# Attention, routing and a sparse expert layer on one core: the last twelve attention tiles are moved into the leading expert's first run

## The chip, the core and the metric

The kernel runs on one NeuronCore of a Trainium2 chip. Its engines run side by side, each through its own queue of instructions in order: TensorE (PE; weight loads, PEld, overlap its matmuls), VectorE (DVE), ScalarE (ACT), GpSimd (POOL) and SyncE (SP, which here only issues DMAs). They wait for one another through semaphores. The metric is the time of one execution in microseconds; the time before is 616.67 us, the median of three runs (615.66 to 618.85).

## What is computed

The reference, shortened:

```python
# q, k, v: (8 batches, 8 heads, 576 tokens, 64), all float32
kv  = einsum('bhsd,bhse->bhde', k, v)
out = einsum('bhsd,bhde->bhse', q, kv)
x   = out / sqrt(mean(out**2, -1) + 1e-6) * g_norm   # then (4608 tokens, 512)
logits = x @ w_gate                                  # 8 experts
e_idx  = argmax(logits, axis=1)
gate   = softmax(logits)[e_idx];  eom = sigmoid(x @ w_output_gate)[e_idx]
y = gate * eom * (relu(x @ w1[e_idx]) @ w2[e_idx])   # w1: 512 x 1024, w2: 1024 x 512
```

Linear attention without a softmax, a normalisation for each head, and an expert layer in which every token goes to one expert.

## The kernel before

Tokens are worked on in 36 tiles of 128 (4.5 tiles to a batch). For each batch b, `kv_part` multiplies k and v in five pieces of rows (four of 128, loaded as `kvm`, and one of 64, `rem`), `kvT_part` transposes the result, and `m_part` multiplies it with the gate weights, so that a tile's product gives outputs and gate logits at once. `out_tile(g)` multiplies q of a tile with this (16 small matmuls in the trace for a tile in one batch, 32 for one that spans two), in a PSUM buffer of the pool `ps_b` (two buffers). ACT copies it out three times: `xrow` (the row for the expert layer), `sq` (squares) and `gp` (logits). `run_out` calls `out_tile` and, for the tile before, `sums` (DVE adds the squares); it then lets each routing generator that is under way go on by a step (`advance`).

`route(gi)` is such a generator, one for each group of tiles. On DVE it takes the root of the mean squares, scales and sums the logits, finds the expert and the gate; on PE it counts positions (`rps`); on DVE, ACT and POOL it builds one-hot places (`la`, `rrc`); on PE it adds them to tables of token numbers (`tblps`). The group that ends at tile 24 also names the expert with most tokens so far, the leading expert (`lead_expert`), and makes its list of rows (`lead_rows`, DVE).

Rows go to a table `xs` in DRAM (`xrow`, and the scales as `xtail`). An expert's run gathers its rows by index (`gather`, POOL), scales the heads (`scale_heads`, on POOL or DVE by `NORMS`), transposes them (`stage`: PE `tps`, ACT and DVE copy to `xT`), and multiplies with w1 (`mm1`, eight blocks `f` of 128 hidden units in `hps`, a buffer of `ps_b`; ACT and DVE write `hT`) and w2 (`mm2`, one output tile of 24 matmuls in `yps`). Each float32 operand is split into a high and a low part (`split`: ACT or DVE writes `whi`, DVE or POOL `wlo`), and a product is three matmuls.

The first run (run 0) takes the leading expert's 384 first rows, out of tiles 0 to 23, so that it can start before the routing is over; run 1 takes the rest of that expert (320 rows), runs 2 to 8 the other experts. Up to the end of the routing the order on each engine is that of the program (`manual_schedule` with `MAN`). It is set by hand: `p1_main` goes through the batches, `HOOKS` inserts steps after certain tiles and `TAIL` gives the steps after the last tile. Letters: R one routing step, L one step of the lead run (`lead_run`: a split, three `stage`, a split, eight `mm1`), S a split of w2, G the gather of run 0, Q the last sums. Before, all loads of attention come first on SP, in slots of 512 KB (30 slots, three kept spare, which `xrow` shares); tile 35 is finished before the lead run's transposes, and run 0's output tiles follow in the main loop, with `stage` of run 1 between their matmuls. Where PE, ACT and DVE are in the main loop, SP's and POOL's order is set by the scheduler.

Of the kernel before, what the change touches and what calls it, by code (L numbers as in the profile page):

```python
# [45 lines left out]
GR = (10, 10, 4, 12)  # L46
# [15 lines left out]
SPARE = 3  # L62
# [18 lines left out]
NORMS = ("PPP", "VPVP")  # L81
# [49 lines left out]
MAN = {ET.PE, ET.Activation, ET.DVE, ET.Pool}  # L131
# [3 lines left out]
def body(ctx: ExitStack, tc: tile.TileContext, kvm, rem, qT, wg, gn, w1, w2, kc, xs, tab, out):  # L135
# [30 lines left out]
    free = list(range(SLOTS))  # L166
    held = {}

    def take(shape, dt, name):
# [157 lines left out]
    def mm2(i, k, events):  # L327
# [5 lines left out]
        ps = ps_y.tile([P, DM], F32, name="yps", tag=f"y{ny % 2}")  # L333
        ny += 1
# [18 lines left out]
        y = hp.tile([P, DM], F32, name="y", bufs=3)  # L353
# [11 lines left out]
        tc.add_to_no_dep_group("out", i_.ins)  # L365

# [81 lines left out]
    def load(spare):  # L448

        while loads and len(free) > spare:  # L450
            where, k, src = loads.pop(0)
            n = src.shape[0]
            if k in where:
                nc.sync.dma_start(out=where[k][P - n:], in_=src)
                continue
            t = take([P] + list(src.shape[1:]), F32, "ld")
            nc.sync.dma_start(out=t[:n], in_=src)
            where[k] = t

    def kv_part(b):  # L460
# [4 lines left out]
        for s in range(5):  # L465
            for p in range(NP):
# [9 lines left out]
        for c in range(4):  # L476
            give(kvt.pop((b, c)))
        if b % 2:
            give(rt.pop(b // 2))
# [3 lines left out]
        return cp  # L483
# [31 lines left out]
    def out_tile(g):  # L515
# [19 lines left out]
        for p in range(NP):  # L535
            for b, r0, m in parts:
                q0 = g % 2 * P + r0

                for u in range(2):
                    r = slice(u * D, (u + 1) * D)  # L540
                    nc.tensor.matmul(ps[r0:r0 + m, u, p * W:(p + 1) * W], qt[g // 2][r, p, q0:q0 + m],  # L541
                                     augs[b % 3][r, p, :], start=True, stop=True)
# [29 lines left out]
    def route(gi):  # L572
# [10 lines left out]
        def pause(k):  # L583
            for _ in range(WAITS.get((gi, k), 1)):
                yield 1
# [179 lines left out]

    def xwrite(g, o, i):
# [30 lines left out]
    def run_out(limit):  # L797
        nonlocal done_tiles
        if done_tiles < limit:
# [4 lines left out]
            advance()  # L804
            load(SPARE)
            if not loads and not opened[0]:
                open_rows(0)
            if lead_placed and opened[0] and (0, 1, 0) not in raw and (1, 0) not in wgt:
                for c in range(1):
                    wload(0, 1, c)  # L810
            for step in HOOKS.get(done_tiles, ""):
                act(step)

    def act(step):
        if step == "R":
            advance()
        elif step == "W":
            for c in range(4):
                wload(0, 2, c)
        elif step == "X":  # L820
            open_rows(1)
# [3 lines left out]
        elif step == "G":  # L825
            gather(0)
            behind.append(nc.gpsimd.memset(mark, 0.0))
            for c in range(1, 4):
                after_rows(wload(0, 1, c))
        elif step == "N":  # L830
            scale_rows(0)
        elif step == "S":
            next(lead2, None)
        else:
            next(lead, None)

    def p1_main():
        load(SPARE)
        for b in range(B):
            lim = tiles_ready(b - 1) if b else 0  # L840
            cp = kv_part(b)
            load(SPARE)
            run_out(lim)
            kvT = kvT_part(cp)
            run_out(lim)
# [4 lines left out]
        while done_tiles < NT:  # L850
            run_out(NT)
        for step in TAIL:
            act(step)
# [319 lines left out]
```

## Time and profile before

| | us |
|---|---|
| median of the runs | 616.67 (615.66 to 618.85) |
| the profiled execution | 620.81, its span 618.8 |
| PE busy in the span | 566.5 (92%), mean granted clock 0.931 |
| DVE, ACT, POOL busy | 263.2, 222.0, 164.0 |
| loads of q, k, v on SP | first 90 us or so, at about 400 GB/s |
| leading expert's gather, first matmul of run 0, first matmul of run 1 | 110.86, 122.74, 174.69 |

A row of the timeline has the start, the duration, the engine, the line of the program, the operation, output and inputs, the shape and a count of merged instructions; in brackets the idle time of the engine ahead of it and what ended that. The granted clock is the share of TensorE's full clock. Spans on POOL are rough. A float32 matmul appears as two in the counts of the trace.

### The profile page before, as it was taken

Reading aid. Unit: us, or ns where it says so; the run is one execution under the profiler, and the core shown is the slowest. Engines: PE = TensorE matmul, PEld = TensorE weight load, DVE = VectorE, ACT = ScalarE, POOL = GpSimd, SP = SyncE. Lnnn points to the kernel's source line nnn. Section 1 sums busy time; section 2 is a strip of 40 time slices with the busy share of each in tenths; the row PEclk is TensorE's granted clock in tenths of the full one; section 3 lists DMA queues with packets and bytes.
Section 4 is the critical chain, followed back from the end, with each engine's and each line's share of the span. In section 5 each row is a group of like instructions: output and inputs, shape, how many; then the busy total and the mean of one; then the engine's idle time right before and its main releaser. Section 6 shows DMA issues by size and latency. Waiting matters only on the chain.

```text
span 618.8 us, 10459 instructions
## 1 busy us (share of the span) xinstructions
PE 566.5 (92%) x4179; PEld 506.3 (82%) x4179; DVE 263.2 (43%) x536; ACT 222.0 (36%) x413; POOL 164.0 (27%) x163
## 2 busy tenths in 40 slices
PE   3799978848999999999899999999999999999991
PEld 3688868747898998889789988998799889889881
DVE  2123688699425456225331453235135325424300
ACT  1335545634225334323331343234234423523310
POOL 2001044443832510630036117104500630110010
PEclk9958777579999999999999999999999999999996
DMA  8999991770564622349776332524432451110010
GB/s 271 367 409 407 405 366 49 246 285 7 166 231 138 202 89 90 87 169 35 16 159 199 115 122 91 172 69 138 145 112 74 135 181 68 53 52 2 0 47 14
DMA packets 39122, 92.53 MB, mean 150 GB/s; under 512 B 14418, under 2 KB 14546, under 8 KB 39072
## 3 DMA queue, kind: packets, MB, share of 16 engines
q1 hardware_dynamic: 32176, 71.63, 37.4%
q0 software_dynamic: 6464, 20.00, 10.2%
q8 instruction: 34, 0.56, 0.4%
q10 hardware_dynamic: 432, 0.21, 0.1%
q14 instruction: 16, 0.13, 0.1%
HBM read 72.63 MB, written 19.99 MB: 150 GB/s over the span
## 4 chain that ended last, share of the span: by engine, by line
PE 57%; issue 19%; DMA 10%; DVE 4%; POOL 3%; ACT 3%; another core or an unknown queue 2%; SPq 0%; POOLq 0%; DVEq 0%
PE hps L308 24%; PE yps L350 23%; PE ops L541 3%; PE kvps L474 3%; DMA ld<-kvm 3%; DMA xs<-xrow 2%; PE tps L271 2%; POOL out L361 2%; DMA ld<-qT 2%; DMA ld<-rem 2%; PE yps L345 1%; POOL xg L239 1%; DMA wraw<-w 1%; DMA xg<-xs,gidx 1%
## 5 line engine op out<-in xcount | busy, mean ns | idle before, releaser
L308 PE MATMUL hps<-xT,whi 128*128 128x320 f32 (+4 forms) x1024 | 197.3, 310 | 9.5 <-DVE hT L318 8.4
L350 PE MATMUL yps<-whi,hT 128*128 128x512 f32 (+2 forms) x592 | 195.9, 399 | 1.0 <-ACT whi L221 1.0
L308 PEld LDWEIGHTS hps<-xT,whi 128*128 128x128 f32 x1024 | 163.6, 191 | 11.9 <-DVE hT L318 9.1
L350 PEld LDWEIGHTS yps<-whi,hT 128*128 128x128 f32 (+2 forms) x592 | 111.3, 188 | 25.2 <-ACT whi L221 1.2
L308 PE MATMUL hps<-xT,wlo 128*128 128x320 f32 (+4 forms) x512 | 121.6, 309 | 0.0
L318 DVE SCALAR_TENSOR_TENSOR hT<-hps,hT 128x512 fp32r<-128x512 f32 (+5 forms) x112 | 59.2, 529 | 142.6 <-ACT hT L317 142.3
L350 PE MATMUL yps<-wlo,hT 128*128 128x512 f32 (+2 forms) x296 | 116.6, 394 | 0.8 <-DVE wlo L224 0.8
L317 ACT ACTIVATE hT<-hps 128x512 fp32r<-128x512 f32 (+5 forms) x112 | 52.5, 469 | 164.0 <-PE hps L308 121.6
L308 PEld LDWEIGHTS hps<-xT,wlo 128*128 128x128 f32 x512 | 89.0, 191 | 0.0
L361 POOL DMA_INDIRECT out<-y,oidx x42 | 44.8, 1068 | 154.2 <-ACT y L360 107.2
L239 POOL DMA_INDIRECT xg<-xs,gidx x42 | 43.2, 1029 | 137.5 <-PE tps L271 54.6
L350 PEld LDWEIGHTS yps<-wlo,hT 128*128 128x128 f32 (+2 forms) x296 | 55.7, 188 | 12.1 <-DVE wlo L224 1.1
L217 DVE SCALAR_TENSOR_TENSOR wlo<-wraw,gcol,whi 128x1024 fp32r<-128x1024 f32 x32 | 43.9, 1372 | 39.6 <-ACT whi L214 39.6
L247 POOL TENSOR_TENSOR xg<-xg 128x512 f32<-128x512 f32 (+3 forms) x40 | 44.0, 1102 | 43.9 <-DMA xg<-xs,gidx 43.5
L541 PE MATMUL ops<-aug,ld 64*128 64x80 f32 (+1 forms) x640 | 49.0, 327 | 5.8 <-ACT gp L549 5.7
L541 PEld LDWEIGHTS ops<-aug,ld 64*128 64x128 f32 (+1 forms) x640 | 44.5, 230 | 8.8 <-ACT gp L549 6.4
L360 ACT ACTIVATE y<-yps,tl 128x512 f32<-128x512 f32 (+2 forms) x37 | 25.5, 689 | 71.4 <-PE yps L350 68.4
L276 ACT CAST xT<-tps 128x512 fp32r<-128x512 f32 (+3 forms) x45 | 23.6, 530 | 67.6 <-PE tps L271 63.9
L277 DVE TENSOR_TENSOR xT<-tps,xT 128x512 fp32r<-128x512 f32 (+3 forms) x45 | 27.7, 617 | 46.9 <-ACT xT L276 43.3
L474 PE MATMUL kvps<-ld 128*64 128x64 f32 (+1 forms) x640 | 36.4, 300 | 11.1 <-DMA ld<-kvm 10.7
L474 PEld LDWEIGHTS kvps<-ld 128*64 128x64 f32 (+1 forms) x640 | 33.1, 209 | 14.0 <-DMA ld<-kvm 12.0
L224 DVE TENSOR_TENSOR wlo<-wraw,whi 128x1024 fp32r<-128x1024 f32 x28 | 34.3, 1226 | 13.5 <-ACT whi L221 6.7
(158 smaller groups left out, 403.2 us busy)
## 6 DMA issues: line engine op xcount, KB each, us to landing
wraw<-w SPq DMA_DIRECT2D x64, 512.0 KB, 3.2
ld<-kvm SPq DMA_DIRECT2D x32, 512.0 KB, 10.2
ld<-qT SPq DMA_DIRECT2D x18, 512.0 KB, 10.2
xs<-xrow SPq DMA_DIRECT2D x13, 512.0 KB, 10.4
xs<-xrow SPq DMA_DIRECT2D x2, 1280.0 KB, 15.2
ld<-rem SPq DMA_DIRECT2D x3, 512.0 KB, 10.2
xg<-xs,gidx POOLq DMA_INDIRECT x42
out<-y,oidx POOLq DMA_INDIRECT x42
```

Source lines behind the costliest of these rows:

```text
L217: eng.scalar_tensor_tensor(out=lo, in0=r, scalar=gcol[:, 0:1], in1=hi.bitcast(F32), op0=ALU.mult, op1=ALU.subtract)
L224: eng.tensor_tensor(out=lo, in0=r, in1=hi.bitcast(F32), op=ALU.subtract)
L239: nc.gpsimd.indirect_dma_start(out=x[:M, :], out_offset=None, in_=rows, in_offset=bass.IndirectOffsetOnAxis(ap=gidx[:M, p, t:t + 1], axis=0))
L247: eng.tensor_tensor(out=v, in0=v, in1=f, op=ALU.mult)
L277: nc.vector.tensor_tensor(out=lo[:, :, c0:c0 + M], in0=v, in1=hi.bitcast(F32)[:, :, c0:c0 + M], op=ALU.subtract)
L308: nc.tensor.matmul(ps[:, j, :n], w[:, o:o + P], x[d][:, j * N:j * N + n], start=(d == 0 and k == 0), stop=(d == 3 and k == 2))
L317: nc.scalar.activation(hh, x, AF.Relu)
L318: nc.vector.scalar_tensor_tensor(out=v(h[:, l:l + n]), in0=x, scalar=0.0, in1=hh.bitcast(F32), op0=ALU.max, op1=ALU.subtract)
L350: nc.tensor.matmul(ps[:M], a, b, start=(f == 0 and k == 0), stop=(f == 7 and k == 2))
L361: i_ = nc.gpsimd.indirect_dma_start(out=out, out_offset=bass.IndirectOffsetOnAxis(ap=oidx[:M, p, t:t + 1], axis=0), in_=y[:M], in_offset=N ...
L474: nc.tensor.matmul(ps[u * D:(u + 1) * D, p * D:(p + 1) * D], k, v, start=(s == 0 and p == 0), stop=(s == 4 and p == NP - 1))
L541: nc.tensor.matmul(ps[r0:r0 + m, u, p * W:(p + 1) * W], qt[g // 2][r, p, q0:q0 + m], augs[b % 3][r, p, :], start=True, stop=True)
```

## The change

The first 24 tiles and batches 0 to 5 go through `p1_main` as before, but `kv_part` stops after the second and the fourth piece of rows and a tile is put there. Only their loads come first; the others (`later`) are issued between the row writes and then at the letters d and f of a new `SCRIPT`. This string takes the place of `HOOKS` and `TAIL` after tile 23: F finishes all routing that is open, 1 and 2 load pieces of w1 and w2, K, T, M are the three steps of a batch's kv product, o is one tile, X opens the row writes of tiles 24 and on, Y is one output tile of run 0. The groups of tiles are 8, 8, 8, 12 instead of 10, 10, 4, 12. Rows of tiles 0 to 23 have twelve slots of their own (`ROWS`), and the loads get the other 18 with none spare. Every tile is multiplied in pieces of 64 rows. Scaling of group 0's logits moves from POOL to DVE (`GPSIMD_GROUPS`), so does the scaling of run 0's rows (`NORMS`); the last group's logits are scaled and summed in halves (`APART`). Run 0's outputs use `ps_b` and slots; SP's order is also that of the program.

```diff
-GR = (10, 10, 4, 12)
+GR = (8, 8, 8, 12)
-SPARE = 3
+ROWS = LEAD_TILES // 2
-HOOKS = {15: 'R', 27: 'RR', 28: 'R', 31: 'RGW', 32: 'X', 34: 'NL'}
-TAIL = "QLLLLRRRSLSRRSLLRRRLSLRRSRLSLL"
-WAITS = {(0, 2): 3, (1, 7): 2, (1, 2): 0, (1, 8): 2, (1, 5): 0, (0, 8): 2, (0, 6): 2}
-GPSIMD_GROUPS = 1
-APART = (2,)
+FIRST = LEAD_TILES
+SCRIPT = ("fQF" "1G1" "K" "L" "T" "LLL" "dd" "1" "M" "L" "dd" "L" "Xo1o" "dd" "L" "o" "o" "dd" "L" "o" "dd" "o" "L" "K"
+          "22" "L" "T" "o" "22" "L" "M" "o" "S" "o" "o" "S" "o" "L" "S" "o" "o" "S" "Q" "L" "R" "L" "RR" "YRRR" "YRRR" "YRRRRRR")
+GPSIMD_GROUPS = 0
+APART = (2, 3)
-NORMS = ("PPP", "VPVP")
+NORMS = ("VVV", "VPVP")
-MAN = {ET.PE, ET.Activation, ET.DVE, ET.Pool}
+MAN = {ET.PE, ET.Activation, ET.DVE, ET.Pool, ET.SP}
-    free = list(range(SLOTS))
+    free = list(range(SLOTS - ROWS))
+    xfree = list(range(SLOTS - ROWS, SLOTS))
...
     def mm2(i, k, events):
-        ps = ps_y.tile([P, DM], F32, name="yps", tag=f"y{ny % 2}")
+        if i == 0:
+            ps = ps_b.tile([P, 2, 512], F32, name="yps0", tag="big")[:, 0]
...
     def kv_part(b):
         for s in range(5):
+            if s in (2, 4):
+                yield
...
     def out_tile(g):
-                for u in range(2):
-                    r = slice(u * D, (u + 1) * D)
-                    nc.tensor.matmul(ps[r0:r0 + m, u, p * W:(p + 1) * W], qt[g // 2][r, p, q0:q0 + m],
+                for c0 in range(r0, r0 + m, D):
+                    for u in range(2):
+                        r = slice(u * D, (u + 1) * D)
+                        nc.tensor.matmul(ps[c0:c0 + D, u, p * W:(p + 1) * W], qt[g // 2][r, p, q0:q0 + D],
...
     def route(gi):
         def pause(k):
-            for _ in range(WAITS.get((gi, k), 1)):
-                yield 1
+            yield 1
...
     def act(step):
+        elif step == "F":
+            while routing:
+                advance()
...
     def p1_main():
-        for b in range(B):
-            lim = tiles_ready(b - 1) if b else 0
-            cp = kv_part(b)
+        for b in range(B - 2):
+            lim = min(tiles_ready(b - 1) if b else 0, FIRST)
+            kv = kv_part(b)
+            for _ in range(2):
+                next(kv)
+                load()
+                run_out(lim)
...
-        while done_tiles < NT:
-            run_out(NT)
-        for step in TAIL:
+        while done_tiles < FIRST:
+            run_out(FIRST)
+        for step in SCRIPT:
             act(step)
...
             if i == 0:
                 gather(1)
                 scale_rows(1)
-                for _ in lead:
-                    next(lead2, None)
-                for _ in lead2:
-                    pass
+                for h in hT[0]:
+                    give(h)
+                for x in range(len(tiles_of(1))):
+                    stage(1, x)
+                continue
```

How the order on the engines moves, at three places. First, PE at the start of the lead run. Before, the last tiles (`ops`, here the end of tile 31 and tiles 32 to 35) stand ahead of run 0's transposes (`tps`) and first block (`hps`):

```order
L541 MATMUL ops<-aug_115,ld 64x80 x2
L541 MATMUL ops<-aug_116,ld 64x80 x2
L541 MATMUL ops<-aug_116,ld 128x80 x32
L271 MATMUL tps<-ident,xg 128x128 x12
L308 MATMUL hps<-xT,whi 128x384 x2
L308 MATMUL hps<-xT,wlo 128x384
```

After, the third group's table matmuls (`tblps`), the seventh batch's kv product and its transposes stand there:

```order
L767 MATMUL tblps<-rrc,la 128x96
L492 MATMUL kvps<-ld 64x64 x40
L507 MATMUL kvTps<-ident,kvc 128x128 x2
L274 MATMUL tps<-ident,xg 128x128 x12
L519 MATMUL mps<-gw,kvT 64x16 x8
L311 MATMUL hps<-xT,whi 128x384 x2
L311 MATMUL hps<-xT,wlo 128x384
```

Tiles 24 to 35 have moved behind the first block. On DVE at the same place, before, with the last index step of the routing (`oidx`), sums of squares (`ss`), the first split and the first tile's copies (`tl`, `xT`):

```order
L900 SCALAR_TENSOR_TENSOR oidx<-gif,zf 128x3
L562 TENSOR_REDUCE ss<-sq 128x8 x3
L216 TENSOR_SCALAR whi<-wraw,gcol 128x1024
L217 SCALAR_TENSOR_TENSOR wlo<-wraw,gcol,whi 128x1024
L562 TENSOR_REDUCE ss<-sq 128x8 x3
L267 COPY tl<-xg 128x1
L277 TENSOR_TENSOR xT<-tps,xT 128x2x128 x2
```

and after:

```order
L951 SCALAR_TENSOR_TENSOR oidx<-gif,zf 128x3
L500 COPY kvc<-kvps 128x256
L219 TENSOR_SCALAR whi<-wraw,gcol 128x1024
L220 SCALAR_TENSOR_TENSOR wlo<-wraw,gcol,whi 128x1024
L250 TENSOR_TENSOR xg<-xg 128x512
L270 COPY tl<-xg 128x1
L280 TENSOR_TENSOR xT<-tps,xT 128x2x128 x2
```

The sums have gone, the kv copy and the scaling of the gathered rows (`xg`, line 250) have come in. Second, PE at the last group's tables. Before, in the middle of run 0's first output tile (`yps`), with two blocks behind them:

```order
L350 MATMUL yps<-whi,hT 128x512 x2
L350 MATMUL yps<-wlo,hT 128x512
L350 MATMUL yps<-whi,hT 128x512
L749 LDWEIGHTS la
L749 MATMUL tblps<-rrc,la 128x96
```

After, the end of the tables is followed by run 0's third output tile:

```order
L767 LDWEIGHTS la
L767 MATMUL tblps<-rrc,la 128x96
L356 MATMUL yps_2252<-whi,hT 128x512
L356 MATMUL yps_2252<-wlo,hT 128x512
L356 MATMUL yps_2252<-whi,hT 128x512 x2
```

The tables have moved from the first output tile to between the second and the third. Third, the start of run 1. Before, its transposes stand between the matmuls of run 0's output tiles, behind run 0's last block:

```order
L308 MATMUL hps<-xT,whi 128x384 x2
L308 MATMUL hps<-xT,wlo 128x384
L271 MATMUL tps<-ident,xg 128x128 x4
L350 MATMUL yps<-whi,hT 128x512
L350 MATMUL yps<-wlo,hT 128x512
```

After, PE has them behind the last output tile:

```order
L356 MATMUL yps_2252<-whi,hT 128x512
L274 MATMUL tps<-ident,xg 128x128 x8
L274 MATMUL tps<-ident,xg 128x64 x4
L311 MATMUL hps<-xT,whi 128x320 x2
L311 MATMUL hps<-xT,wlo 128x320
```

and POOL's queue there, from the last group's places on, with gathers (`xg<-xs`) for runs 1 and 2, the scaling (line 250) and the third output tile's write (`out`):

```order
L737 TENSOR_SCALAR la<-ni,rlon 128x128 x4
L242 DMA xg<-xs,gidx 128x528 x2
L242 DMA xg<-xs,gidx 64x528
L242 DMA xg<-xs,gidx 128x528 x2
L250 TENSOR_TENSOR xg<-xg 128x512
L242 DMA xg<-xs,gidx 128x528
L367 DMA out<-y_2277,oidx 4608x512
```

Nothing of run 0 stands between run 1's transposes and its first block any more.

More of the change, by code (lines that the diff above doesn't have):

```diff
@@ L352, in mm2 @@
                 e()
-        y = hp.tile([P, DM], F32, name="y", bufs=3)
+        y = take([P, DM], F32, "y0") if i == 0 else hp.tile([P, DM], F32, name="y", bufs=3)
         if M == T:
@@ L365, in mm2 @@
         tc.add_to_no_dep_group("out", i_.ins)
+        if i == 0:
+            give(y)
     def lead_run():
@@ L446, in body, with load, fetch @@
                 nq += 1
[L448 to L458, printed above, removed]
+    cut = lambda w, k: (k if w is qt else 2 * k if w is rt else k[0])
+    later = [l for l in loads if cut(l[0], l[1]) >= (FIRST // 2 if l[0] is qt else FIRST * P // S + 1)]
+    loads = [l for l in loads if not any(l is x for x in later)]
+    later.sort(key=lambda l: (12.5 + (l[1] - FIRST // 2) // 2 if l[0] is qt else 2 * l[1] + 0.1 if l[0] is rt else 2 * l[1][0]))
+    def load():
+        while loads and free:
+            fetch(loads)
+    def fetch(loads):
+        where, k, src = loads.pop(0)
+        n = src.shape[0]
+        if k in where:
+            nc.sync.dma_start(out=where[k][P - n:], in_=src)
+            return
+        t = take([P] + list(src.shape[1:]), F32, "ld")
+        nc.sync.dma_start(out=t[:n], in_=src)
+        where[k] = t
     def kv_part(b):
@@ L475, in kv_part @@
                                      stop=(s == 4 and p == NP - 1))
[L476 to L479, printed above, removed]
+            if s < 4:
+                give(kvt.pop((b, s)))
+            elif b % 2:
+                give(rt.pop(b // 2))
         nc.scalar.copy(augs[b % 3][:, :, 0:D], ps[:, 0:NP * D].rearrange("q (p d) -> q p d", p=NP))
@@ L803, in run_out @@
                 sums()
-            advance()
-            load(SPARE)
+            if done_tiles <= FIRST:
+                advance()
+            load()
             if not loads and not opened[0]:
                 open_rows(0)
[L808 to L812, printed above, removed]
+            elif opened[0] and done_tiles <= FIRST and done_tiles % 2 == 0 and len(later) > LATER:
+                fetch(later)
+    w1s, w2s = list(range(4)), list(range(4))
+    state = {"b": B - 2}
     def act(step):
+        b = state["b"]
         if step == "R":
             advance()
[L817 to L821, printed above, removed]
+        elif step == "F":
+            while routing:
+                advance()
         elif step == "Q":
@@ L849, in p1_main @@
                 run_out(lim)
-        while done_tiles < NT:
-            run_out(NT)
-        for step in TAIL:
+        while done_tiles < FIRST:
+            run_out(FIRST)
+        for step in SCRIPT:
             act(step)
+        assert not later and done_tiles == NT and not w1s and not w2s and state["y"] == len(tiles_of(0))
         while routing:
             advance()
+        for _ in lead:
+            assert False
+        for _ in lead2:
+            assert False
     vec = nc.vector
@@ L1061, in body @@
                 mm2(i, k, at.get(k, {}))
-            if i == 0:
-                for h in hT[0]:
-                    give(h)
-            if i > 0:
-                for c in range(4):
-                    drop(2, c)
+            for c in range(4):
+                drop(2, c)
     main.close()
```

52 lines of the change are left out of this document (39 added, 13 removed).

## The prediction

> **What bounds the kernel now.** I read the stretches first (us: busy PE, PEld, DVE, ACT, POOL with counts; granted clock, DMA share, GB/s). They are cut where tile 23's square is done, where the leading expert's gather starts (110.9), where its first matmul starts (122.7) and where the second run's first matmul starts. The left-out row is 87.2 to 110.9. The second fence is the row of that matmul.
>
> ```profile
> 0.00:87.20 87.20, 68.83 (x1142) 61.75 (x1143) 32.73 (x84) 35.95 (x95) 12.05 (x18) 0.80 1.00 373
> ...
> 110.90:122.70 11.80, 9.76 (x74) 8.65 (x72) 8.17 (x15) 7.42 (x20) 7.26 (x7) 0.50 0.86 277
> 122.70:174.90 52.20, 41.52 (x209) 36.15 (x210) 36.76 (x81) 17.07 (x32) 28.95 (x24) 0.89 0.49 160
> 174.90:618.80 443.90, 428.45 (x2480) 383.17 (x2478) 164.31 (x270) 150.18 (x236) 108.24 (x102) 0.98 0.37 103
> ```
>
> ```profile
> 174.69 0.45 PE L308 MATMUL hps<-xT,whi 128*128 128x320 f32 x2
> ```
>
> From 174.9 on PE is busy 428.45 of 443.9 us, on work that the change leaves alone. So the question is when the second run's first matmul comes: at 174.69 now. Ahead of it PE is idle 10.7 us in the lead run (52.20 - 41.52), and 18.4 us in the first stretch, whose DMA share is 1.00. The change trades these holes for others. I follow the chain that ends in that matmul through five links.
>
> **Link 1, attention to tile 23.** Rows of ACT, PE, PEld and SP, a line of the waits (total, times, longest) and one of the issues (us to landing):
>
> ```profile
> 86.16 0.59 ACT L546 COPY xrow<-ops 128x512 f32<-128x512 f32 x1 [0.31 <-PE ops L541]
> 87.28 0.62 ACT L546 COPY xrow<-ops 128x512 f32<-128x512 f32 x1
> 79.56 4.07 PE L474 MATMUL kvps<-ld 128*64 128x64 f32 x77
> PE ops L541 <- ACT gp L549: 3.9, 5, 1.0
> 83.52 0.72 PE L541 MATMUL ops<-aug,ld 64*64 64x80 f32 x30
> 84.99 2.02 PE L541 MATMUL ops<-aug,ld 64*128 64x80 f32 x32
> 109.02 1.10 PEld L541 LDWEIGHTS ops<-aug,ld 64*64 64x64 f32 x32
> 110.29 5.20 PEld L541 LDWEIGHTS ops<-aug,ld 64*128 64x128 f32 x48 [0.17 <-issue]
> 50.07 2.89 SPq L457 DMA_DIRECT2D ld<-qT  x3
> ld<-qT SPq DMA_DIRECT2D x18, 512.0 KB, 10.2
> ```
>
> The first two rows are ACT's copies of tiles 23 and 24; tile 23 is through ACT by 87.2. The seventh batch's kv product (4.07, and 0.3 for its transposes) moves behind it: -4.4. Tiles set between the pieces of each kv product hide most of the 3.9 us in which PE's tiles wait for ACT: -3.0. Every tile takes the 64-row form that tile 22 has: 32 small matmuls in 0.8 us (30 take 0.72) against 1.01 (half of 2.02); at half clock 1.10 against 1.73 (a third of 5.20). The mean clock is 0.80, so two fifths of the time at half: 0.36 a tile, and -6.1 for the 17 tiles that don't wait for loads. Tile 23 is done at 73.7. Bounds: 82.8 if only the kv product goes; below, the loads of q that tiles 22 and 23 need are issued from 50.07 on and take 10.2, and some 7.5 us of kv and tile work follow: 67.8. The row writes now alternate with loads on SP's queue, where a write waits for its tile; what it can hold up is the seventh batch, not needed before link 3.
>
> **Link 2, the third group's routing, alone.** Now tiles 24 to 35 hide it. After, its matmuls stand on PE's queue ahead of the next kv product, so PE waits for DVE's chain. DVE's rows for the last group (twelve tiles), DVE's first step after the table matmuls of the present third group, and the gather on POOL:
>
> ```profile
> 134.76 1.76 DVE L618 TENSOR_TENSOR gp<-gp,xtail 128x1536 f32<-128x1536 f32 x1
> 138.09 2.80 DVE L622 TENSOR_REDUCE lg<-gp 128x192 f32<-128x1536 f32 x1
> 140.93 0.25 DVE L632 TENSOR_REDUCE mx<-lg 128x12 f32<-128x96 f32 x1
> 144.39 0.25 DVE L668 TENSOR_TENSOR rog<-ohb,lg 128x96 f32<-128x96 bf16 x1
> 146.12 0.16 DVE L704 TENSOR_TENSOR cnt<-rps,cf 128x8 f32<-128x8 f32 x1
> 147.72 0.75 DVE L729 TENSOR_TENSOR rrc<-cf,rhk 128x576 bf16<-128x576 f32 x1
> 150.08 0.18 DVE L742 TENSOR_TENSOR xtail<-rdn 128x12 f32<-128x12 f32 x1
> 109.13 0.26 DVE L890 TENSOR_TENSOR t<-tblps,perm 128x96 f32<-128x96 f32 x1 [0.41 <-PE tblps L749]
> 110.86 1.08 POOL L239 DMA_INDIRECT xg<-xs,gidx  x1 [5.09 <-DVE oidx L900]
> ```
>
> Small steps come every 0.25 us (0.25 busy at twelve tiles). For eight tiles, an estimate from these rows: the last square's sum and the rest of the second group 2.8; nine steps 2.3; scaling 1.3 and sums 2.0 (two thirds of 1.76 and 2.80, and two instructions for one); mask and its count 1.6; gate and slots 1.7 (146.12 - 144.39); leading expert, seven steps, 1.6; places 2.0 (2.4 at twelve, 147.72 to 150.08); table matmuls 0.6; table to gather 1.7 (110.86 - 109.13). Sum 17.6, bounds 15 and 20. Gather at 91.3, against 110.86.
>
> **Link 3, gather to first matmul**, 11.9 us now (110.86 to 122.74):
>
> ```profile
> 114.06 0.92 DVE L216 TENSOR_SCALAR whi<-wraw,gcol 128x1024 fp32r<-128x1024 f32 x1
> 124.63 1.28 DVE L217 SCALAR_TENSOR_TENSOR wlo<-wraw,gcol,whi 128x1024 fp32r<-128x1024 f32 x1 [0.62 <-ACT whi L214]
> 158.01 0.69 DVE L247 TENSOR_TENSOR xg<-xg 128x512 f32<-128x512 f32 x1 [1.66 <-DMA xg<-xs,gidx]
> 121.19 1.08 PE L271 MATMUL tps<-ident,xg 128*128 128x128 f32 x4 [1.62 <-DVE xT L277]
> 123.58 0.42 DVE L277 TENSOR_TENSOR xT<-tps,xT 128x256 fp32r<-128x256 f32 x1 [0.44 <-ACT xT L276]
> 122.74 1.15 PE L308 MATMUL hps<-xT,whi 128*128 128x384 f32 x2 [0.46 <-ACT xT L276]
> ```
>
> DVE will do in order: the copy of the kv product (on PE beside the gather; done some 3.5 us into it), the split (0.92 + 1.28), then three times scale, wait for the transposes, subtract. The scaling moves from POOL, where it ran ahead, onto this chain: 0.69 + (124.00 - 121.19) = 3.5 us a tile at half clock. 3.5 + 2.2 + 10.5 = 16.2, less 1.2 since the first matmul needs only half of the last tile's copies (122.74 against 124.00): 15.0, bounds 12 and 17. The first weight load is behind the third group's row tails on SP and lands inside these 3.5 us. First matmul at 106.3, 16.4 us earlier than now.
>
> **Link 4, the lead run with twelve tiles and the last kv product in it,** to the end of tile 35:
>
> ```profile
> 126.88 0.63 PE L308 MATMUL hps<-xT,whi 128*128 128x384 f32 x2
> 145.08 0.51 PE L308 MATMUL hps<-xT,whi 128*128 128x384 f32 x2
> 147.16 0.39 PE L350 MATMUL yps<-whi,hT 128*128 128x512 f32 x1
> ```
>
> PE: the first block of hidden units at half clock 4.1 (122.74 to 126.88), six more at 2.08 (145.08 to 147.16) 12.5, twelve tiles at 0.85 10.2, kv product, transposes and small product 4.7: 31.5. Tiles, blocks and small products share two PSUM buffers, so each waits until the job before the last is copied out. ACT needs 1.12 a tile (87.28 - 86.16), and its six splits stand between, each about as long as DVE's 1.28. Laid out job by job this leaves 4.9 us of holes; I add 1.0 for a clock that dips in the stretch of four tiles: 37.4, bounds 33 and 50. Tile 35 ends at 143.7. The last kvm loads wait on SP behind the rows of tiles 24 and 25, and have some 10 us until PE wants them.
>
> **Link 5, tile 35 to the second run.** Now most of the lead run's matmuls cover it; after, one block and three output tiles:
>
> ```profile
> 125.61 2.55 POOL L224 TENSOR_TENSOR wlo<-wraw,whi 128x1024 fp32r<-128x1024 f32 x1 [6.75 <-ACT whi L221]
> 125.83 2.39 DVE L589 TENSOR_SCALAR ra<-ss 128x96 f32<-128x96 f32 x1
> 161.93 5.48 PE yps L350 x24
> 154.18 3.80 DMA xg<-xs,gidx
> 129.00:137.00 8.00, 0.28 (x2) 0.00 (x0) 7.79 (x9) 1.92 (x3) 4.66 (x2) 0.81 0.81 296
> 137.00:140.50 3.50, 3.46 (x11) 3.46 (x12) 3.50 (x2) 0.00 (x0) 0.00 (x0) 0.50 0.00 0
> ```
>
> From tile 35's end: ACT and DVE drain, 3.7; the chain's first step sits beside POOL's last split and takes 2 us more, as at 125.83; routing at twelve tiles by the rows of link 2, 2.3 + 1.8 + 2.8 + 1.4 + 1.7 + 1.6 + 2.4 = 14.0; table matmuls 0.3; to the gather 2.0. That is 22.0. PE meanwhile has the last block (2.1) and two output tiles of 5.48, then waits some 6 us for the table matmuls, which stand ahead of the third output tile. That tile covers 5.5 us of what follows: POOL scales the middle tile behind five gathers (6.2, more than the 3.8 in which the first rows land), 1.1; transposes and copies 1.8; then the last tile is scaled on DVE, 0.7, and copied, 1.4. Together 33.2, bounds 28 and 38: second run at 176.9. PE has been idle some 8 us by then; after the idle 8.0 at 129 the clock was 0.50 for 3.5 us, which costs 1.7. So 178.6 against 174.69: **+3.9 us**. At nothing I put the rows' own slots and the lead output's shared buffers: loads are limited by the DMA share of 1.00, not by slots, and no tile wants a buffer beside the output.
>
> The profiled execution took 620.81 (span 618.8), 4.1 above the median of 616.67; I carry the difference over to the median: 620.6.
>
> **Rivals.** (a) Attention keeps the pace of the loads, because PE, fed without holes, gets the full clock. For it: the smaller form and the tiles between kv pieces. Against: PE was busy 9.76 of 11.80 us from 110.9, mostly with tiles, at 0.50. Tile 23 then ends at 67.8 (-5.9) and the dip in link 4 goes (-1.0): 613.7, faster. It decides only if tile 23 is done by about 68. [...]
> (b) Link 5 is covered better: the chain escapes POOL's split (-2.0) and the middle tile is scaled before the later gathers (-2.6): 616.0, no change. Against it: those gathers stand first on POOL's queue.
> (c) The clock stays at half through link 4: six blocks at 4.1 for 2.08, +12: 632.7. For it the same row at 0.50; against it 0.89 in the present lead run.
> (d) The lead run starts no earlier, so the change doesn't do what it says: row writes land late and hold the gather until 110. They are 6.3 MB behind 20 MB of loads, at 373 GB/s done near 75, so I give it little; link 1 to 3's 16.4 us lost: 637.
>
> **How the numbers follow.** My sum 42%, its own range 616 to 626; (a) 22%, (b) 20%, (c) 13%, (d) 3%. Half a per cent, 3.1 us, is about what a measurement here can tell from no change. Faster: most of (a), a third of (b): 0.27. Within: the rest of these and a third of my sum, which ends close to that line: 0.28. Slower: 0.45. For 8 in 10 the range goes past (a) to 609 and short of (c) to 631.
>
> **What would show it.** Tile 23 through ACT near 74; PE idle some 15 us behind it with DVE busy; gather near 91; first lead block near 106; tile 35 near 144; holes of about 6 us ahead of the third output tile and 8 behind it; second run near 177, and from there to the end the length of now. I am wrong if tile 23 comes by 68, if the lead run is at half clock, or if the stretch behind the second run's start changes.

## The result, and the profile after

| | before | after |
|---|---|---|
| median of the runs, us | 617.76 | 636.16 (632.48 to 637.32) |
| ratio after to before | | 1.0285, 95% interval 1.0225 to 1.0346 |
| the profiled execution, its span | 620.81, 618.8 | 637.32, 635.4 |
| mean granted clock | 0.931 | 0.937 |

The change makes the kernel 18.4 us slower; the forecast was 3.9 us, with a range that ended at 631. (All ratios below are against runs of the kernel before on the same chip and leave out runs more than 1.5% above the fastest of their kernel, five of twelve in early_tiles_2 and three of ten in early_tiles_4, whose medians over all runs are 616.77 and 611.39 against 616.75 and 617.75 before.)

First the stretches of the changed kernel, in the columns of the prediction's first fence (stretch and its length; busy PE, PEld, DVE, ACT, POOL with counts; granted clock, DMA share, GB/s). They are cut at the links' ends: tile 23's square, the leading expert's gather, run 0's first matmul, tile 35's last matmul, run 1's first matmul. The last line is the kernel before between its tile 23 and its gather, which the prediction left out.

```profile
0.00:82.70 82.70, 56.83 (x1385) 48.71 (x1385) 36.10 (x98) 35.22 (x93) 8.38 (x15) 0.86 0.98 355
82.70:100.90 18.20, 6.07 (x83) 5.02 (x85) 15.46 (x66) 3.10 (x12) 7.79 (x11) 0.56 0.17 43
100.90:114.50 13.60, 5.61 (x60) 4.04 (x56) 6.10 (x14) 2.61 (x7) 3.30 (x4) 0.63 0.88 306
114.50:151.10 36.60, 30.49 (x570) 26.43 (x566) 14.92 (x23) 22.85 (x51) 4.49 (x2) 0.94 0.60 216
151.10:187.70 36.60, 23.74 (x123) 19.23 (x123) 23.29 (x73) 10.21 (x22) 19.51 (x19) 0.90 0.51 162
187.70:635.40 447.70, 431.36 (x2480) 386.10 (x2480) 165.09 (x271) 149.69 (x235) 112.67 (x107) 0.98 0.37 99
```
```profile
87.20:111.00 23.80, 18.06 (x280) 16.66 (x281) 21.29 (x88) 11.53 (x35) 7.61 (x13) 0.69 0.41 118
```

The rows of the timeline that end the links, in order:

```profile
82.13 0.61 ACT L567 ACTIVATE sq<-ops 128x512 f32<-128x512 f32 x1
100.90 1.08 POOL L242 DMA_INDIRECT xg<-xs,gidx  x1 [4.94 <-DMA xs<-xtail]
150.29 0.78 PE L560 MATMUL ops<-aug,ld 64*64 64x80 f32 x32
174.66 1.08 POOL L242 DMA_INDIRECT xg<-xs,gidx  x1 [4.72 <-DVE oidx L951]
187.74 1.09 PE L311 MATMUL hps<-xT,whi 128*128 128x320 f32 x2 [0.46 <-ACT xT L279]
```

Run 1's first matmul is at 187.74, 13.05 us later than before (174.69). Behind it the changed kernel takes 447.7 us (635.4 - 187.74), the kernel before 444.1 (618.8 - 174.69): 3.55 more, which makes the 16.6 us between the two spans. Run 1's first block, dense matmuls, runs at half clock (0.50 granted) until 193.70, which costs 3.0 us of these; the same stretch took 441 to 448 us in the twelve kernels below, so a microsecond or two in it means little.

What fills the 13.05 us is idle TensorE. Up to run 1 as a whole it is idle 65.0 us for 36.8, and busy 122.7 for 138.1. From tile 23 to run 1 it is idle 18.2 - 6.07, 13.6 - 5.61, 36.6 - 30.49 and 36.6 - 23.74, in sum 39.1 us. Before, from 87.2 to 174.9, it was 5.7, 2.0 and 10.7, in sum 18.5. Ahead of tile 23 it was idle 18.4 us before and is 25.9 now.

By the prediction's links:

| link | predicted length (bounds for its end) | measured | miss |
|---|---|---|---|
| 1, attention to tile 23 | 73.7 (67.8 to 82.8) | 82.7 | +9.0 |
| 2, third group's routing | 17.6 | 18.2 | +0.6 |
| 3, gather to first matmul | 15.0 | 13.6 | -1.4 |
| 4, lead run to tile 35 | 37.4 | 36.6 | -0.8 |
| 5, tile 35 to run 1 | 33.2 | 36.7 | +3.5 |
| behind run 1's start | +1.7 | +3.55 | +1.9 |

Together these misses are 12.8 us, of the 14.5 that lie between +3.9 and +18.4; the rest is that the two profiled spans are 16.6 apart and the medians 18.4. Links 1 and 5 carry the miss, much of it in waits that the trace of before did not show. Here are link 1's waits, a line each for who waited for whom (total us, times, longest), up to 83 us:

```profile
PE kvps L492 <- DMA ld<-kvm: 8.6, 6, 5.4
PE ops L560 <- issue: 4.7, 3, 2.1
PE ops L560 <- ACT gp L568: 2.9, 3, 1.1
PE kvTps L507 <- DVE kvc L500: 2.5, 3, 1.1
PE tblps L767 <- POOL la L737: 1.7, 5, 0.4
```

The second line is new: TensorE stops inside a tile and waits for nothing that the profile shows, three times, 2.15, 2.04 and 0.46 us. I call such a stop, in a tile or in a batch's kv matmuls, a hole. The last line is a wait that `WAITS` had kept away: the first group's table matmuls stand on TensorE's queue while GpSimd still writes their places.

### The profile page after: what moved, and what is told of

It is laid out like the page before. It is cut to its first block, busy times and chain, and to the rows that moved or that the text cites. A ratio compares the mean times of both kernels' runs of the same rounds, so it can differ in the third digit from the quotient of the medians.

```text
span 635.4 us, 11490 instructions
## 1 busy us (share of the span) xinstructions
PE 554.1 (87%) x4691; PEld 489.5 (77%) x4691; DVE 261.0 (41%) x543; ACT 223.7 (35%) x417; POOL 156.1 (25%) x156
## 4 chain that ended last, share of the span: by engine, by line
PE 57%; issue 19%; DVE 6%; POOL 5%; DMA 5%; ACT 4%; another core or an unknown queue 1%; POOLq 0%; ACTq 0%; SPq 0%; DVEq 0%
PE hps L311 27%; PE yps L356 20%; PE kvps L492 3%; PE tps L274 3%; PE ops L560 2%; POOL out L367 2%; DMA ld<-kvm 2%; DMA ld<-qT 2%; POOL xg L242 1%; DMA wgs<-wg 1%; PE yps L351 1%; ACT sq L567 1%; ACT xrow L565 1%; POOL la L737 1%
## 5 line engine op out<-in xcount | busy, mean ns | idle before, releaser
L366 ACT ACTIVATE y<-yps,tl 128x512 f32<-128x512 f32 (+2 forms) x37 | 25.5, 689 | 82.2 <-PE yps L356 79.2
L250 POOL TENSOR_TENSOR xg<-xg 128x512 f32<-128x512 f32 (+3 forms) x37 | 40.6, 1101 | 40.7 <-DMA xg<-xs,gidx 40.4
L560 PE MATMUL ops<-aug,ld 64*64 64x80 f32 x1152 | 35.3, 263 | 14.0 <-ACT gp L568 5.0
L560 PEld LDWEIGHTS ops<-aug,ld 64*64 64x64 f32 x1152 | 28.4, 155 | 19.2 <-issue 10.0
L492 PE MATMUL kvps<-ld 128*64 128x64 f32 (+1 forms) x640 | 34.6, 283 | 8.8 <-DMA ld<-kvm 8.6
L274 PE MATMUL tps<-ident,xg 128*128 128x128 f32 (+3 forms) x168 | 26.7, 283 | 15.0 <-issue 5.9
```

Source lines behind the costliest of these rows:

```text
L250: eng.tensor_tensor(out=v, in0=v, in1=f, op=ALU.mult)
L274: nc.tensor.transpose(ps[:, c, :M], x[:M, c * P:(c + 1) * P], ident[:M, :M])
L492: nc.tensor.matmul(ps[u * D:(u + 1) * D, p * D:(p + 1) * D], k, v, start=(s == 0 and p == 0), stop=(s == 4 and p == NP - 1))
L560: nc.tensor.matmul(ps[c0:c0 + D, u, p * W:(p + 1) * W], qt[g // 2][r, p, q0:q0 + D], augs[b % 3][r, p, :], start=True, stop=True)
```

## Experiments on link 1

A link's end below is that of one profiled execution. Three kernels have the changed kernel's attention to the letter (the changed one, middle_tile_dve and weights_behind): tile 23 came at 82.7, 84.4 and 84.2. So a difference under 2 us in one such row says little.

**late_table.** The table matmuls of group 0 two tiles later:

```diff
+WAITS = {(0, 8): 3}
         def pause(k):
-            yield 1
+            for _ in range(WAITS.get((gi, k), 1)):
+                yield 1
```


> The changed kernel with one edit: the first group's table matmuls go onto TensorE's queue two attention tiles later, so that GpSimd's eight places (5.2 us) are done when TensorE comes to them. Theory 1 (the holes of link 1 are several separate waits, this one costs 2.6 us of idle TensorE between 65.7 and 68.8): tile 23 through ACT at 80.1 instead of 82.7, the second run at 185.1 instead of 187.7, the time 2.6 us shorter. Rival (TensorE waits for the loads or for ACT right behind it, so the wait only moves): tile 23 still at 82 to 83, time within 1 us.

Ratio 1.0287 (1.0255 to 1.0319), as the changed kernel. Tile 23 came at 80.9, run 1 at 184.90, both near theory 1's figures, and the wait for GpSimd's places is gone; but the time is not shorter, and the holes went from 4.7 us to 10.4 (six of them). Here are three, with the stretch from one to the next:

```profile
47.48 0.77 PE L561 MATMUL ops<-aug,ld 64*64 64x80 f32 x28 [1.77 <-issue]
53.78 0.50 PE L561 MATMUL ops<-aug,ld 64*64 64x80 f32 x15 [1.93 <-issue]
59.84 0.69 PE L561 MATMUL ops<-aug,ld 64*64 64x80 f32 x10 [2.36 <-issue]
```
```profile
47.48:53.78 6.30, 3.84 (x128) 3.23 (x127) 5.16 (x15) 2.79 (x8) 0.00 (x0) 1.00 1.03 407
53.78:59.84 6.06, 3.70 (x127) 3.24 (x127) 2.57 (x8) 2.76 (x7) 0.23 (x1) 0.96 1.04 390
59.84:72.54 12.70, 11.30 (x254) 9.64 (x253) 9.32 (x26) 7.12 (x20) 4.62 (x8) 0.61 1.07 379
```

From hole to hole TensorE runs 128, 128 (127 recorded) and 256 (254) matmuls, each with its weight load, in 6.30, 6.06 and 12.70 us. In all five stretches between its holes it is a multiple of 128 matmuls, and never less than 6 us for 128 (the other two took 12.19 us for 256, 255 recorded, and 6.65 for 128). The changed kernel's three holes stand 255 (256) and 128 matmuls apart, in 12.46 and 6.22 us. In the first two stretches above, TensorE is busy only 3.84 and 3.70 us. The wait that was taken out came back in part, as the rival had it, but neither loads nor ACT took its place: this pace did.

**rows128.** The tile product as before the change:

```diff
-                for c0 in range(r0, r0 + m, D):
-                        nc.tensor.matmul(ps[c0:c0 + D, u, p * W:(p + 1) * W], qt[g // 2][r, p, q0:q0 + D],
+                        nc.tensor.matmul(ps[r0:r0 + m, u, p * W:(p + 1) * W], qt[g // 2][r, p, q0:q0 + m],
```


> The changed kernel with the tile product as before the change, in pieces of up to 128 rows (16 small matmuls for a tile in one batch, not 32). Theory 1 (the 64-row form shortens a tile's matmuls by 0.36 us as the prediction's term of -6.1 has it, but its twice as many instructions arrive too slowly while the loads saturate the DMA engines: the two holes of 2.1 us and one of 0.5 in which TensorE waited for nothing shown): those holes vanish (-4.6), the matmuls grow by some 6, tile 23 1 to 2 us later than 82.7, time within 3 us of the changed kernel. Rival (the holes have another cause, and the term of -6.1 holds in full): holes stay, tile 23 near 89. Second rival (the form gains nothing because TensorE's time there is covered): tile 23 near 78, time 4 us shorter.

Ratio 1.0344 (1.0301 to 1.0386). Tile 23 at 84.4, no matmul that waited for nothing shown, and TensorE busy 64.65 us up to 83 against 56.83. So TensorE's busy time fell by 7.8 us; the tiles' own matmuls went from 32.30 us to 26.05, which is 6.25, the size of the prediction's term (6.1). Tile 23 gained 1.7 of it. Theory 1 holds as far as the form makes the holes: in all traces of this study with the 128-row form up to tile 23 TensorE has no such hole in the attention ahead of 83 us, and in all with the 64-row form there are two or more. The queues of the two traces (packets, MB, share), up to 83 us:

```profile
q8 instruction: 8, 0.13, 0.6%
```
```profile
q8 instruction: 11, 0.18, 0.9%
```

The first line is rows128, the second the changed kernel. A packet of this queue is 16 KB (0.18 MB in 11). Over the whole program the 64-row form has 512 matmuls more, each with its weight load, and the queue moves 38 packets for 34, here and in before_rows64 against the kernel before: 128 matmuls to a packet, an estimate from these counts, which fits the holes. Up to 83 us the form has 336 matmuls more (21 tiles, 32 for 16; three span two batches and have 32 in both forms), which is 2.6 packets; three more are seen here, two in before_rows64 (10, for 8 in the kernel before).

**whole_kv.** No tiles between the pieces of a kv product:

```diff
-            if s in (2, 4):
-                yield
...
-            for _ in range(2):
-                next(kv)
-                load()
-                run_out(lim)
```


> The changed kernel with each kv product in one piece again (no tiles between its pieces of rows). The prediction's term: tiles between the pieces hide 3.0 us of waits for ACT, so tile 23 comes 3 us later than 82.7. Theory 1 (the waits only change place, TensorE's waits for ACT in the changed kernel are 2.9 us against 3.9 before): within 1.5 us of 82.7, time within 1.5 us.

Ratio 1.0265 (1.0237 to 1.0293). Tile 23 at 83.0, 0.3 us later than in the changed kernel; holes of 6.0 us in all. The term of -3.0 is worth nothing that shows; theory 1 had it so.

**before_rows64.** The 64-row form alone, in the kernel before; the diff is that of rows128 the other way round.

> The kernel before with one edit, the tile product in pieces of 64 rows, one part of the change alone. Prediction's term taken over: 0.36 us for each tile that does not wait for loads, 17 up to tile 23 (-6.1) and 12 behind it (-4.3): tile 23 near 81, time 5 to 10 us shorter. Theory 1 (new holes from instructions that arrive late eat most of it while the loads run, up to about 75 us; the last tiles gain): holes of some 2 us without a releaser in the attention, tile 23 at 85 to 88, time 1 to 4 us shorter. Rival: slower, since the holes cost more than the shorter matmuls save: 2 us longer.

Ratio 0.9988 (0.9969 to 1.0008): no change. Tile 23 came at 84.6 for 87.2, run 1 at 169.90 for 174.69; there were holes of 6.7 us up to 83, and one of 3.02 at 87.09. Theory 1's row for tile 23 holds; its gain in time is not to be seen, and the profiled execution, with run 1 4.8 us earlier, was the fastest of twelve.

**before_mixed_form.** The 64-row form from tile 24 on only (`D_ = D if g >= LEAD_TILES else P`).

> The kernel before with tiles 24 to 35 alone in the 64-row form, tiles 0 to 23 as they were. Theory 1: the tiles behind 24 lie behind most of the loads, so the shorter form costs no holes there: no or small holes without a releaser, tile 35 through ScalarE some 3 us before 118.8, time 1 to 3 us shorter than before. Rival: ScalarE's three copies of 1.5 us a tile set the pace of those tiles, so nothing changes: within 1 us of before.

Ratio 0.9969 (0.9942 to 0.9995): some 0.3% faster, with no hole; tile 35 was through ACT at 112.9 for 118.8, more than theory 1 had. Here, and in before_rows64 behind its loads, these stretches of TensorE are among the fastest:

```profile
105.00:112.00 7.00, 5.60 (x188) 4.62 (x180) 6.06 (x17) 6.06 (x16) 2.69 (x3) 0.76 0.49 128
```
```profile
105.00:112.00 7.00, 5.73 (x176) 4.56 (x168) 4.80 (x13) 6.46 (x17) 4.31 (x5) 0.76 0.64 172
```

188 and 176 matmuls in 7 us are 128 in 4.8 and 5.1 us, without a hole, at DMA shares of 0.49 and 0.64. That alone tells nothing of the pace: in whole_kv, from 40 to 52 us, 324 matmuls pass in 12 us (128 in 4.7) without a hole at a share of 1.02, so a short stretch can be faster than the pace from hole to hole. Over 18 us (92 to 110) the two kernels here ask for 128 in 5.9 and 6.1 us, no more than that pace.

**less_load.** The loads of k and v of batches 2 to 5 are left out (their products take batch 1's):

```diff
-        loads += [(kvt, (b, c), kvm[b][:, c]) for c in range(4)]
+        if not 2 <= b < 6:
+            loads += [(kvt, (b, c), kvm[b][:, c]) for c in range(4)]
```


> The changed kernel with the loads of k and v of batches 2 to 5 left out (the products of these batches use batch 1's k and v, so the computation is another one); instructions and their order are those of the changed kernel, 8 MB of the loads fall away. Theory 1 (TensorE's instructions come in packets of 16 KB, 128 matmuls each, and while the loads saturate the DMA engines a packet takes about 6.2 us): with the DMA engines less than full behind 30 us, the holes without a releaser in the attention shrink to under 0.5 us each and tile 23 comes 8 us or more before 82.7. Rival (TensorE takes in instructions at a pace of its own, 128 matmuls in some 6.2 us whatever the DMA engines do): the holes stay or grow, since it waits less for data; then 128 matmuls still take 6 us or more between them.

Tile 23 came at 79.5, not 8 us early. The loads that stay only moved ahead, so the DMA engines were still busy to 50 (a share of 0.93):

```profile
30.00:50.00 20.00, 13.26 (x436) 11.52 (x433) 10.68 (x22) 10.77 (x29) 0.00 (x0) 0.90 0.93 339
50.00:60.00 10.00, 9.10 (x236) 8.07 (x236) 4.84 (x16) 5.80 (x18) 0.00 (x0) 0.68 0.56 197
```

In the first stretch, at a share of 0.93, there are two holes of 2.87; in the second, at 0.56, 236 matmuls in 10 us (128 in 5.4) and no hole there or later in the attention. This does not decide between the two causes. Between the two holes (35.91 to 48.08) 255 matmuls pass in 12.17 us, the same pace, though the share there is only 0.86; and behind 50 us the demand is not above it (522 matmuls from 50 to 75, 128 in 6.1). Whether the loads or TensorE's own intake set the pace stays open. The one execution took 624.98 us, with run 1 at 182.03.

## Experiments on link 5

**middle_tile_dve.** `NORMS = ("VVV", "VVVP")`.

> The changed kernel with one edit: the middle tile of run 1 is scaled on VectorE, not on GpSimd behind five gathers. Prediction's rival (b), its second half: 2.6 us less in link 5. From the trace of the changed kernel, where that tile is scaled at 182.50 on GpSimd and its transposes start at 183.60: second run's first matmul 2 to 4 us earlier behind the gather (9 to 11 us, not 13.1). Rival (the rows themselves land late, since 14 weight loads run beside the gathers): 12 to 13 us behind the gather as now, no gain.

Ratio 1.0284 (1.0245 to 1.0324). Run 1 starts 12.4 us behind its gather (176.44 to 188.80) for 13.1: the rival's answer. VectorE now waits for the rows themselves, 0.5 and 0.4 us.

**weights_behind.** The weight loads of run 2 wait for run 1's gathers:

```diff
         raw[(p, which, c)] = r
+        if p:
+            for n in rows1:
+                tc.add_manual_dep(d.ins, n, ...)
```


> The changed kernel with one edit: the weight loads of run 2 wait on SyncE until the three gathers of run 1 have landed. In the changed kernel 14 weight loads are issued from 172.75 on, two microseconds ahead of the gathers at 174.66, and the DMA share is 0.88 to 0.98 from there to 190; in the run with the middle tile on VectorE the third gather, issued at 179.09, is waited for until 186.82, 7.7 us. Theory 3 (the gathered rows share the DMA engines with the weights): each gather lands in some 3.6 us, the first matmul of the second run comes 9.5 to 11 us behind the first gather instead of 13.1, the time 2 to 3 us shorter. Rival (GpSimd's scaling behind five gathers and VectorE's chain set the pace): 12.5 to 13.1 us behind it as now.

Ratio 1.0257 (1.0212 to 1.0302), not told apart from 1.0285 by time. The rows of the trace, GpSimd's first gather and run 1's first matmul:

```profile
177.08 1.07 POOL L248 DMA_INDIRECT xg<-xs,gidx  x1 [4.73 <-DVE oidx L959]
188.25 1.10 PE L319 MATMUL hps<-xT,whi 128*128 128x320 f32 x2 [0.46 <-ACT xT L287]
```

11.2 us (188.25 - 177.08), 1.9 less than in the changed kernel, just short of theory 3's 9.5 to 11. But it is not shown that the edit did it: late_table, rows128 and less_load, whose weight loads are issued 1.9 us ahead of the gather as in the changed kernel, took 11.2, 11.4 and 11.2 as well; whole_kv took 13.4. What sets the groups apart in the traces is the granted clock in the 4 us behind that gather, 0.77 to 0.84 in the four kernels with 11.2 to 11.4 and 1.00 in the three with 12.4 to 13.4.

## Experiments on the uncovered routings

**early_tiles.** If idle TensorE beside the two routings is the loss, work has to be put there. The new script (9: squares pile up; q: one square's sum; the other letters as before), with tiles up to 23 in the 128-row form, the first split's high part on ACT, the third output tile in the main loop behind `gather(1)` with run 1's `stage` inside, `NORMS = ("VPP", "VVV")` and the group-0 table two tiles later:

```diff
-SCRIPT = "fQF1G1KLTLLLdd1MLddLXo1oddLooddLoddoLK22LTo22LMoSooSoLSooSQLRLRRYRRRYRRRYRRRRRR"
+SCRIPT = "fddddddddddQ9RRKRRoRRoRToMRoRoF1G11qqKqqoToMLLoLoLX1qqL2oqL2oq2LoLQR2LSRRLSRLSRLSRRLRYRRY"
```


> The changed kernel, its script rewritten: tiles 24 to 28 and the kv product of batch 6 go onto TensorE between the routing steps of the third group, tiles 29, 30 and the kv product of batch 7 beside the gather, tiles 31 to 35 between the transposes and the first two blocks of the lead run; the loads behind tile 24 are issued ahead of that routing; their squares are added in the wait for the gather; the third output tile stands behind the gather of run 1 with that run's transposes inside; rows of runs 0 and 1 are scaled by V, P, P and V, V, V; tiles up to 23 in the 128-row form; the first group's table matmuls two tiles later. Theory 2 (what the change lost behind link 1 is TensorE idle beside two routings that nothing covers, 12 us in link 2, 8 in link 3, 13 in link 5): tile 35 ends near 120 instead of 151, its routing runs beside the lead run, the gather of run 1 comes at 145 to 150 and the second run starts at 155 to 165; time 600 to 610. Rival (the tiles hold up VectorE's and ScalarE's steps of the routing as much as they fill TensorE): leading expert's gather 6 us or more later than 98 to 104, second run at 175 or later, time 618 or more.

Two of run 0's three row tiles were not scaled in this kernel (step N is missing), some 2 us of GpSimd's work (1.04 a tile in the changed kernel). Ratio 0.9981 (0.9957 to 1.0005): the changed kernel's 2.8% are gone. Lead gather at 104.2, tile 35 through ACT at 128.2, run 1's gather at 160.59 and its first matmul at 173.03: both expectations are half right. Link 5's chain took 32 us; that VectorE's routing steps and the lead run's `hT` steps now wait for each other is my reading of it.

**early_tiles_2.** N is in, and VectorE's waits are mended; `lead_run` does its first `stage` ahead of its first split:

```diff
+SCRIPT = "fddddddddddQ9RRRRRRKRoToMoRoRoF1GN11qqKqqoToMLLLoLoX1qqLo2Loq2oQR2LRR2LRSLRSLRSLSLRLRYRRY"
-PLACES = ['P', 'P', 'PAV', 'PAV', 'PAV']
+PLACES = ['P', 'PAV', 'PAV', 'PAV', 'PAV']
```


> The kernel early_tiles put right (there the scaling of the rows of two of run 0's three tiles was missing, so it was some 2 us short of work on GpSimd) and with other places for what held up its routing: the kv product of batch 6 goes behind the third group's first six steps on VectorE, not behind two (VectorE stood 5.6 us in that wait); the split of the first weights goes behind the first transposes; the last four squares are added at once behind tile 35 (it took 6.8 us from tile 35's square at 128.3 to the first step of the last routing at 135.1); the second group's places go to three engines. Theory 2: gather of run 0 near 99 to 101 (104.2), first lead block near 112 to 114 (119.2), tile 35 near 123, run 1's gather 148 to 153, second run at 160 to 166 and a time of 603 to 611. Rival (VectorE's and ScalarE's work is the bound of this stretch, so every step moved ahead delays another): run 1's gather at 156 or later, time 614 to 618.

Ratio 0.9945 (0.9903 to 0.9988). In the profiled execution (611.39 us, the second fastest of twelve) every mark is where theory 2 put it, or ahead: lead gather 99.04, run 1's gather 153.29, run 1 at 164.68. The median of its runs, 616.77, lies in the rival's range. Its tile 23 came at 75.7; the next two kernels, with the same attention, had it at 82.2 and 82.4. The granted clock from 40 to 60 was 0.84 and 1.00 here and 0.50 in those two, and the same 1049 matmuls kept TensorE busy for 56.9 us here and 63.4 and 64.0 there. In all five kernels of this study with the changed attention in the 128-row form, tile 23 comes 18.4 to 19.7 us above that busy time.

**early_tiles_3.** With weights_behind in it.

> early_tiles_2 and weights_behind in one kernel. Theory 3 with theory 2: 2 to 3 us less than early_tiles_2, since its last output tile of run 0 hides part of the landing only. Rival: the third output tile of run 0 covers the landing of the rows there, no difference beyond 1 us.

Ratio 0.9934 (0.9898 to 0.9971), not told apart from early_tiles_2. Gather to run 1 takes 10.65 us for 11.4: the rival.

**early_tiles_4.** `SPLITS` of w2 from `'AP'` to `'AV'`.

> early_tiles_3 with one edit: the low parts of run 0's four w2 splits are written by VectorE, not by GpSimd. In early_tiles_2 and early_tiles_3 four VectorE steps that stand beside these four GpSimd instructions (2.4 us each) are stretched: 3.99 us for 1.83, 2.92 for 1.28, 2.20 for 0.26, 1.89 for 0.26, 7.4 us in all, on the chain from tile 35 to the gather of run 1. Theory 4 (a VectorE step that meets a GpSimd instruction waits until that one is done, so the work costs VectorE more when GpSimd does it): the four stretched steps go back to their lengths, four new splits of 1.28 come, 2.3 us less from tile 35 to the gather, time 1 to 3 us less than early_tiles_3. Rival (the stretched steps wait beside other waits of the chain): no gain, or 1 to 3 us more, since VectorE gets 5.1 us of work on its chain.

Ratio 0.9864 (0.9829 to 0.9898): faster than early_tiles_3, and than the kernel before by 1.4% (1.0% by the medians of all runs). Against the changed kernel it is 4.1% less (0.9864 / 1.0285). In early_tiles_3 VectorE's scaling of the logits, two steps merged in a row, stands beside GpSimd's low parts:

```profile
130.68 4.00 DVE L649 TENSOR_TENSOR gp<-gp,xtail 128x768 f32<-128x768 f32 x2
131.09 5.81 POOL L232 TENSOR_TENSOR wlo<-wraw,whi 128x1024 fp32r<-128x1024 f32 x2 [19.34 <-ACT whi L229]
```
```profile
130.83 1.83 DVE L649 TENSOR_TENSOR gp<-gp,xtail 128x768 f32<-128x768 f32 x2
```

4.00 us there, 1.83 here. Tile 35 to run 1's gather went from 34.5 us (125.5 to 160.0) to 30.7 (125.65 to 156.34): 3.8 less, where 2.3 were expected. The four stretched steps were 2.2, 1.6, 1.9 and 1.7 us longer in early_tiles_3, a little less than one GpSimd instruction (2.4 us) each. Two of them stand beside a single GpSimd instruction each and end with it, as theory 4 has it: `ohb` at 143.10 for GpSimd's 142.98, `rog` at 146.95 for 146.84. Why VectorE waits there is not shown.

The stretches of early_tiles_4 in the changed kernel's order, tile 23, lead gather, first block, tile 35, run 1's gather, run 1:

```profile
82.40:103.30 20.90, 13.08 (x309) 11.34 (x311) 15.16 (x66) 11.65 (x35) 3.67 (x6) 0.71 0.85 300
103.30:117.30 14.00, 9.40 (x253) 7.78 (x249) 8.51 (x21) 8.53 (x23) 6.19 (x6) 0.87 0.82 262
117.30:125.70 8.40, 7.35 (x84) 6.59 (x85) 4.87 (x7) 5.88 (x12) 0.00 (x0) 0.73 0.57 223
125.70:156.30 30.60, 26.02 (x145) 23.07 (x144) 27.96 (x78) 12.18 (x24) 3.84 (x5) 0.94 0.27 88
156.30:167.00 10.70, 8.92 (x45) 6.85 (x43) 3.45 (x8) 2.92 (x5) 8.50 (x9) 1.00 0.62 195
```

TensorE is idle 7.8, 4.6, 1.1, 4.6 and 1.8 us, in sum 19.9, for 39.1 in the changed kernel. Tile 23 is at 82.4 for 82.7, and run 1 starts at 167.0 for 187.7. So the 20 us that early_tiles_4 is ahead at run 1's start are the idle time beside the routings, shown by filling it. Several edits stand in that kernel at once, so how much each filled is not shown. The other 5 of the difference in span (635.4 to 609.5) lie behind that start, where one execution says little.

## Why the prediction was wrong

**Link 1 is the step that failed.** Of its three terms only the first came true: 87.2 - 4.4 is 82.8, the upper bound, and tile 23 came at 82.7. The term of -6.1 was about right in what it was worked out from: by its own rows it is 0.38 us a tile, 6.4 for 17, and the tiles' matmuls shrank by 6.25 us. Wrong was the step from there to the forecast, that what a tile's matmuls save, tile 23 gains. With the shorter matmuls TensorE is through 128 of them sooner (busy 3.84 us of the 6.30 from hole to hole in late_table), and stops: 4.7 us in the changed kernel, 9.1 and 11.1 in the other two executions of the same attention. That the stop is a wait for the next packet of instructions is argued from the counts; the profile shows no releaser. In tile 23's end 1.7 of the 6.1 is left, no more than the scatter from run to run. The term of -3.0 measured 0.3. And the first group's table matmuls held TensorE 1.7 us for GpSimd's places, which I had put at nothing when `WAITS` went; late_table, where that wait is gone, had tile 23 1.8 us earlier, within the scatter too.

**Link 5** was 3.5 us too short in two places. The chain to the gather took 23.6, not 22.0; of this 1.1 lies between the end of the table matmuls (171.54) and the gather, 3.1 us where I had 2.0. From gather to first matmul it was 13.1 for 11.2: I had priced GpSimd's five gathers (6.2), and in this execution GpSimd then waited 1.53 us more for the middle tile's rows. Four other kernels with the same link took the 11.2 to 11.4 of the sum, three of them with the weight loads as early as here, so what makes the rows late stays open.

**Links 2, 3 and 4** held, within 1.4 us each. The routing alone took 18.2; in this the gather's last index was done at 99.63, and GpSimd waited 1.3 us more, for the write of the row scales (the releaser in its row), which the sum did not have, so its steps were priced 0.7 too high; the three row tiles came 3.5 us apart (tps at 105.90, 109.41 and 112.94); the lead run had its clock at 0.94 and no dip.

**The half clock** at run 1's start cost 3.0 for 1.7: it lasted 6.0 us, not the 3.5 seen at 137 before. In late_table and rows128 the same block had it for 4.1 and 3.6 us (from 184.90 and 188.23, until a pair of its matmuls fell from 0.73 us to under 0.5). What sets its length is not shown.

**The rivals.** (a) is out: tile 23 by 68 did not come, and the clock in the attention was 0.86. (b) is out: the first routing step did meet GpSimd's split (1.39 us, where it takes 0.21 in early_tiles_2), and its second half, tried, gave 0.7 us. (c) is out by the clock of link 4, 0.94. (d)'s 637 is close to the time, and its mechanism is wrong: the gather came 10 us earlier than before, at 100.90, and a late row write held it for 1.3 us only. The agreement is luck.

**The range.** Each link ended inside its own bounds. The range did not hold the time because it was drawn around the rivals and not around the sum: 9.0 and 3.5 us on the high side in two links, which their bounds allowed, take the sum from 620.6 to 633.1, past 631.

What stays open: whether it is the full DMA engines or TensorE's own intake that makes 128 matmuls take 6 us from hole to hole, what made run 1's rows late in link 5, and how much of link 1's scatter is the granted clock.

## What to carry to other kernels

Splitting matmuls into smaller ones is priced by the instructions too (here the tiles' matmuls shrank by 6.25 us, and tile 23 came 1.7 us earlier): count the matmuls from hole to hole, and take 128 in 6 us as the fastest pace from hole to hole that these traces showed; a stretch of 12 us between two holes can be faster (324 matmuls in whole_kv). When work is moved away from beside a chain of small VectorE steps, that chain becomes idle time of TensorE (beside the third group's routing 12.1 of 18.2 us, for 5.7 of 23.8 before); move only what leaves enough behind to cover it, or fill the gap with work that needs neither VectorE nor ScalarE at once. Add up the bounds of a chain's links for its range, not the ends of the rivals.

## What the runs showed of the hardware that I had not expected

By the packet counts (38 for 34 with 512 matmuls more) TensorE's instructions come in packets of 16 KB (0.62 MB in 38) over a DMA queue, and every hole in late_table stands a multiple of 128 matmuls behind the last. One attention code ended at 75.7 us and at 82.4 in two kernels, with a granted clock of 0.84 to 1.00 and of 0.50 in the same 20 us. And a GpSimd instruction of 2.4 us cost VectorE 1.8 on average where it met one of its steps (7.4 us in four, in early_tiles_3), more than the 1.22 that VectorE took for the same work itself in early_tiles_4.
